# One-token attention with a gated feed-forward: how w_down, wo and V's last tiles are loaded

## The chip, the cores and the metric

The kernel runs on one core of one Trainium2 chip. The metric is device time in microseconds (us) of that core. Before the change the median of three runs is 2534.33 us (2534.22 to 2534.78).

## What is computed

One token `x` (512 values, bf16) goes through two branches that are mixed by a scalar gate.

```python
q  = (x @ wq)                        # 32 heads of 128
s  = q . k_cache[h, :, :] * 128**-0.5  # 65536 keys a head
o  = softmax(s) @ v_cache[h]           # [32, 128]
a  = o.reshape(1, 4096) @ wo           # wo: 4096 x 512
b  = (silu(x @ w_gate) * (x @ w_up)) @ w_down   # w_down: 1792 x 512
g  = sigmoid(sum(x * gate_w))
out = g * a + (1 - g) * b
```

K and V hold 32 heads x 65536 x 128 bf16 values each: 512 MiB each. The weights are small beside them: wq 4 MiB, wo 4 MiB, w_gate, w_up and w_down 1.75 MiB each.

## The kernel before

**Tiles.** The caches are read in tiles of 16384 keys (4 MiB, 32 KiB on each of 128 partitions): four K tiles and four V tiles a head, 128 of each in all. Five buffers ("slots") of that size lie in SBUF; `take` hands out the slot that has been free the longest and `give` returns one. K tiles, V tiles and the larger weights all go through these five slots, so the order of `take` and `give` in the program decides which transfer waits for which reader.

**Work on a tile.** For a K tile, VectorE multiplies by the query (L254) and adds halves (L258), TensorE adds the rest up with the identity as weights (`scores`, L267), and VectorE folds that into the scores (L281). After four K tiles a head's maximum and exponentials are made (`row_max`, `exponentials`). For a V tile, TensorE runs 32 matmuls `O_ps<-V_t,P_sb` (`values`, L322), four blocks of 128 keys each. When a head's four V tiles are done, `head_copy` (ScalarE, L335) and `head_turn` (TensorE L351, ScalarE L358) turn the result into a column of `oT`, and `project` (L365) multiplies that with the head's 128 rows of wo into two accumulators `a_ps`. In the last V tile the last eight blocks (`TURNED`) are multiplied the other way round, straight into `oh_ps` (L343), behind everything else.

**Order.** All loads but two tiny ones are issued by SyncE, in the order of the program, with eight completion semaphores that are used in turn. The order at the start is: the first part of wq, K tiles 0, 1, 2, the rest of wq, w_gate, K tile 3, w_up, then six DMAs of w_down, K tile 4, two more DMAs of w_down, V tile 0. From K tile 5 on, a step issues one K and one V tile (`steps`); V is four tiles behind K at first and from K tile 43 on falls back to eight (`LAG`, `SPREAD`), so that the run ends with V tiles alone.

**w_down before (L393 to L412).** It lies on 64 partitions, 28 rows of 512 values on each. It comes in eight DMAs of eight partitions each, and each partition's share is one run of 28,672 bytes. `feed_forward_out` first turns the hidden vector from 128x14 to 64x28 (L227, L231) and then runs 28 matmuls (L233).

**wo before.** Rows of heads 0 to 15 come four heads at a time (512 KB, in runs of 1 KB) in mid-run (`load_wo`, L163), into a pool of two buffers; rows of heads 16 to 31 (2 MB) come behind the last V tile in four DMAs (`load_late`, L169) into a ring slot. Heads 0 to 15 are projected in mid-run, heads 16 to 31 at the very end (L480).

**V's last tiles before.** `V_CUTS` cuts the third last tile and the second last in two DMAs each, and the last in six (32, 32, 32, 16, 8 and 8 blocks).

Of the kernel before, what the change touches and what calls it, by code (L numbers as in the profile page):

```python
# [8 lines left out]
ACT = mybir.ActivationFunctionType  # L9
ALU = mybir.AluOpType  # L10
AXIS = mybir.AxisListType
P = 128
# [3 lines left out]
NB = 128  # L16
# [6 lines left out]
LAG = 8  # L23
SPREAD = 40

WG = 4
LATE = 16
LATE_CUTS = (0, 5, 10, 14, LATE)
TURNED = 8
V_CUTS = {3: (0, 64, NB), 2: (0, 64, NB), 1: (0, 32, 64, 96, 112, NB - TURNED, NB)}  # L30


@with_exitstack
def kernel(
# [14 lines left out]
    nc = tc.nc  # L49
    bf16 = mybir.dt.bfloat16  # L50
    f32 = mybir.dt.float32

    _, H, Sk, Dh = A_k_cache.shape
    D = A_x.shape[2]
    F = B_w_gate.shape[1]
    KT = D // P
    FT = F // P
    G = Sk // (NB * P)
    NBH = Sk // P
    N = H * G  # L60
# [4 lines left out]
    consts = ctx.enter_context(tc.tile_pool(name="consts", bufs=1))  # L65
# [7 lines left out]
    psum_m = ctx.enter_context(tc.tile_pool(name="psum_m", bufs=2, space=bass.MemoryType.PSUM))  # L73
# [7 lines left out]
    def take(name):  # L81
        slot = free.pop(0)
        held[name] = slot
        return ring.tile(
            [P, NB * Dh], bf16, name=name.split(".")[0], tag=f"slot{slot}"
        )

    def give(name):
        free.append(held.pop(name))
# [14 lines left out]
    def load(dst, cache, n, name, cuts=(0, NB), slot=None):  # L104
        h, g = divmod(n, G)
        t = take(f"{name}.{n}") if slot is None else slot
        view = t.rearrange("p (j d) -> p j d", d=Dh)
        src = cache[0, h, g * NB * P : (g + 1) * NB * P, :].rearrange("(p j) d -> p j d", j=NB)
        for a, b in zip(cuts[:-1], cuts[1:]):
            nc.sync.dma_start(out=view[:, a:b, :], in_=src[:, a:b, :])  # L110
        dst[n] = view

    def load_k(n):
        load(K_tiles, A_k_cache, n, "K_t")

    def load_v(n):
        load(V_tiles, A_v_cache, n, "V_t", V_CUTS.get(N - n, (0, NB)))

# [9 lines left out]
    ident_b = consts.tile([P, P], bf16, name="ident_b")  # L128
# [29 lines left out]
    wo_tiles = {}  # L158

    def load_wo(g):  # L160
        wo_tiles[g] = wo_pool.tile([P, WG, D], bf16, name="wo_sb", tag="wo_sb")
        rows = A_wo[g * WG * P : (g + 1) * WG * P, :]
        nc.sync.dma_start(out=wo_tiles[g], in_=rows.rearrange("(h p) n -> p h n", p=P))  # L163

    def load_late(cuts):
        late = take("wo_late.0")[:, : LATE * D].rearrange("p (h n) -> p h n", n=D)
        rows = A_wo[(H - LATE) * P :, :].rearrange("(h p) n -> p h n", p=P)
        for a, b in zip(cuts[:-1], cuts[1:]):
            nc.sync.dma_start(out=late[:, a:b, :], in_=rows[:, a:b, :])  # L169
        return late  # L170

    def feed_forward_in():
        gu_ps = psum_m.tile([P, 2 * FT], f32, name="gu_ps", tag="misc")
        for w in range(2):
            cols = wgu_sb[:, w].rearrange("p t (m c) -> p t c m", c=FT)
            for ft in range(FT):
                for t in range(KT):
                    nc.tensor.matmul(
                        gu_ps[:, w * FT + ft : w * FT + ft + 1],
                        lhsT=cols[:, t, ft, :],  # L180
                        rhs=xT[:, t : t + 1],
                        start=(t == 0),
                        stop=(t == KT - 1),
                    )
        gu_sb = consts.tile([P, 2 * FT], f32, name="gu_sb")
        nc.scalar.activation(out=gu_sb, in_=gu_ps, func=ACT.Copy)
        eg = consts.tile([P, FT], f32, name="eg")
        nc.scalar.activation(out=eg, in_=gu_sb[:, :FT], func=ACT.Exp, scale=-1.0)
        return gu_sb, eg
# [32 lines left out]

    def feed_forward_out(hT, rest):
        b_ps = psum_m.tile([1, D], f32, name="b_ps", tag="misc")
        h_ps = psum_m.tile([HP, GT], f32, name="h_ps", tag="misc")
        for r in range(2):
            nc.tensor.matmul(  # L227
                h_ps[:, r * FT : (r + 1) * FT], lhsT=ident_b[:, r::2], rhs=hT, start=True, stop=True
            )
        h2 = consts.tile([HP, GT], bf16, name="h2")  # L230
        nc.scalar.activation(out=h2, in_=h_ps, func=ACT.Copy)  # L231
        for t in range(GT):
            nc.tensor.matmul(  # L233
                b_ps, lhsT=h2[:, t : t + 1], rhs=wd_sb[:, t, :], start=(t == 0), stop=(t == GT - 1)
            )
        nc.scalar.activation(out=b_sb, in_=b_ps, func=ACT.Copy, scale=rest)
        for i, a in enumerate(a_ps):
            nc.tensor.matmul(  # L238
                a, lhsT=ones_f[0:1, 0:1], rhs=b_sb[:, i * HD : (i + 1) * HD], start=True, stop=False
            )  # L240
# [22 lines left out]
    def scores(n):  # L263
        S = F_tiles[n] = psum_s.tile([P, NB, QUAD], f32, name="S_ps")
        width = width_of(n)
        for c in range(0, width, QUAD):
            nc.tensor.matmul(  # L267
                S,
                lhsT=ident_b,
                rhs=K_tiles[n][:, :, c : c + QUAD],  # L270
                start=(c == 0),
                stop=(c == width - QUAD),
            )
        del K_tiles[n]
        give(f"K_t.{n}")
# [84 lines left out]
        )  # L360

    def project(h):
        rows = wo_tiles[h // WG][:, h % WG, :] if h < H - LATE else wo_late[:, h - (H - LATE), :]
        for i, a in enumerate(a_ps):
            nc.tensor.matmul(  # L365
                a,
                lhsT=oT[:, h : h + 1],
                rhs=rows[:, i * HD : (i + 1) * HD],
                start=False,
                stop=(h == H - 1),  # L370
            )


    def score_tile(n):
        for _ in products(n):
            pass
        if n:
            fold(n - 1)
# [11 lines left out]
    score_tile(1)  # L390
    xs = gate_sum()
    scores(1)
    wd_t = take("wd_t.0")  # L393
    HP = P // 2
    GT = F // HP
    wd_sb = wd_t[:HP, : GT * D].rearrange("p (t n) -> p t n", t=GT)
    wd_rows = B_w_down.rearrange("(p t) n -> p t n", t=GT)
    firsts = (0, 1, 2, 3, 32, 33, 34, 35)

    def load_wd(i):  # L400
        part = slice(firsts[i], firsts[i] + 29, 4)
        nc.sync.dma_start(out=wd_sb[part], in_=wd_rows[part])

    for i in range(6):
        load_wd(i)
    for g in range(1, H // QG):
        queries(g)
    give("wq_t.0")
    eg2 = gate_exp(xs)
    load_k(4)  # L410
    load_wd(6)
    load_wd(7)  # L412
    score_tile(2)
    rest = gate_value(eg2)
    scores(2)
# [7 lines left out]
    v = 0  # L423
# [5 lines left out]
        steps.append((None, v))  # L429
        v += 1  # L430

    done = tot_ps = wo_late = None
    for n, v in steps:
        if n is not None and n > G:
            load_k(n)
        if v is not None:
            if v % (WG * G) == 2 and v // (WG * G) < (H - LATE) // WG:
                load_wo(v // (WG * G))
            if v:
                load_v(v)  # L440
            if v == N - 1:
                wo_late = load_late(LATE_CUTS)
        vector = iter(()) if n is None else products(n)
        top_of = None
        if n is None:
            top_of = H - 1 if F_tiles else None
        elif n % G == 0:
            top_of = n // G - 1
            vector = (i for a in (0, NB // 2) for i in products(n, a, a + NB // 2))
        if top_of is not None:  # L450
            next(vector, None)
            fold(top_of * G + G - 1)
            mT_ps = row_max(top_of)
            next(vector, None)
            exponentials(top_of, mT_ps)
        if n == G:
            hT = feed_forward_mid(*ff)
        for _ in vector:
            pass
        if n is not None and n % G:  # L460
            fold(n - 1)
        if tot_ps is not None:
            weight(*tot_ps)
            tot_ps = None
        if n == G:
            feed_forward_out(hT, rest)
            give("wd_t.0")
        if done is not None:
            head_turn(done, head_copy(done))
        if v is not None:  # L470
            values(v)
        if top_of is not None:
            tot_ps = top_of, total(top_of)
        if n is not None:
            scores(n)
        if done is not None and done < H - LATE:
            project(done)
        done = v // G if v is not None and v % G == G - 1 else None
    head_turn(H - 1, head_copy(H - 1))
    for h in range(H - LATE, H):  # L480
        project(h)

    out_sb = consts.tile([1, D], bf16, name="out_sb")
    nc.vector.tensor_copy(out=out_sb[:, :HD], in_=a_ps[0])  # L484
# [32 lines left out]
```

## Time and profile before

| What | Value |
|---|---|
| Median of three runs | 2534.33 us |
| The profiled execution | 2534.41 us |
| Its span in the profile | 2532.6 us |
| Mean granted TensorE clock | 0.772 |
| Busy: TensorE, VectorE, ScalarE | 61%, 82%, 3% |
| Read from HBM | 1087.64 MB, 429 GB/s over the span |

The span starts with the first recorded instruction and ends with the last; 1.8 us of the profiled execution lie outside it. All bytes are input: the output is 1 KB. The DMA work is spread over 16 DMA engines, and a DMA has landed when each engine that carries a part of it has reported.

### The profile page before, as it was taken

The page shows a single profiled execution, that of the slowest core. Times are in us where ns is not written, and L with a number is a line of the kernel's source. Part 1 is how long each engine was busy: PE and PEld are TensorE (multiplying, and loading weights), DVE is VectorE, ACT ScalarE, POOL GpSimd, SP SyncE. Part 2 cuts the span into 40 slices and gives each one's busy share as a digit, 9 for nine tenths or more (in the row PEclk, how much of TensorE's full clock was granted, in tenths as well). Part 3 has the DMA queues.
Part 4 walks back from the last instruction along what each step waited for, and adds up shares of the span by engine and source line. Part 5 has one row for each costly group of instructions (what it writes and reads, how often), then busy time and mean ns, then how long its engine had stood idle before and what let it go on. Part 6 is the DMA issues. An engine that isn't in the chain of part 4 may idle for free.

```text
span 2532.6 us, 13195 instructions
## 1 busy us (share of the span) xinstructions
PE 1533.7 (61%) x5786; PEld 581.6 (23%) x5786; DVE 2083.7 (82%) x744; ACT 77.7 (3%) x208; POOL 0.9 (0%) x7
## 2 busy tenths in 40 slices
PE   4656656665566555555665566556656665665569
PEld 1222222222222112222222122222222221222223
DVE  7788888888887999988888888888888888888860
ACT  1000000000000000000000000000000000000000
POOL 0000000000000000000000000000000000000000
PEclk9777777777777787787777777777777777777779
DMA  9999999999999999999999999999999999999998
GB/s 412 418 431 433 435 432 430 434 433 432 431 433 434 431 433 434 432 431 434 433 432 433 434 432 432 435 431 432 432 434 432 431 435 433 431 434 433 432 432 351
DMA packets 43915, 1088.49 MB, mean 430 GB/s; under 512 B 4753, under 2 KB 9362, under 8 KB 10258
## 3 DMA queue, kind: packets, MB, share of 16 engines
q1 hardware_dynamic: 43570, 1087.65, 99.7%
q8 instruction: 45, 0.74, 0.1%
q14 instruction: 12, 0.10, 0.0%
q10 hardware_dynamic: 288, 0.00, 0.0%
HBM read 1087.64 MB, written 0.00 MB: 429 GB/s over the span
## 4 chain that ended last, share of the span: by engine, by line
DMA 71%; PE 23%; DVE 4%; issue 1%; ACT 0%; SPq 0%; DVEq 0%
DMA V_t<-in_A_v_cache_dram 63%; PE O_ps L322 21%; DMA K_t<-in_A_k_cache_dram 8%; DVE K_t L254 3%; DVE K_t L258 1%; PE S_ps L267 1%; DMA wo_late<-in_A_wo_dram 0%; PE b_ps L233 0%; DVE S_sb L281 0%; DVE m L287 0%; PE oh_ps L351 0%; PE a_ps L238 0%; ACT P_sb L300 0%; PE a_ps L365 0%; PE mT_ps L291 0%
## 5 line engine op out<-in xcount | busy, mean ns | idle before, releaser
L322 PE MATMUL O_ps<-V_t,P_sb 128*4 128x512 bf16 x4094 | 1154.5, 452 | 663.5 <-DMA V_t<-in_A_v_cache_dram 663.5
L254 DVE TENSOR_TENSOR K_t<-K_t,q_bc 128x16384 bf16<-128x16384 bf16 (+1 forms) x159 | 1117.2, 7026 | 357.9 <-DMA K_t<-in_A_k_cache_dram 346.7
L258 DVE TENSOR_TENSOR K_t<-K_t 128x8192 bf16<-128x8192 bf16 (+1 forms) x314 | 859.7, 2738 | 8.6
L322 PEld LDWEIGHTS <-P_sb 128*4 128x4 bf16 x4094 | 393.0, 97 | 1405.1 <-issue 1064.1
L267 PE MATMUL S_ps<-K_t,ident_b 128*128 128x512 bf16 x1056 | 263.3, 393 | 100.6 <-DVE K_t L258 100.6
L267 PEld LDWEIGHTS <-ident_b 128*128 128x128 bf16 x1056 | 98.0, 101 | 248.0 <-issue 158.0
L291 PE MATMUL mT_ps<-diag,ones_f 128*128 128x128 f32 x64 | 24.5, 483 | 150.1 <-ACT diag L289 150.1
L351 PE MATMUL oh_ps<-ident_f,O_sb 4*128 4x1 f32 x256 | 55.5, 334 | 74.5 <-ACT O_sb L335 74.5
L281 DVE TENSOR_REDUCE S_sb<-S_ps 128x128 f32<-128x512 f32 x128 | 87.5, 683 | 4.9 <-PE S_ps L267 4.9
L289 ACT ACTIVATE diag<-ident_f,m 128x128 f32<-128x128 f32 x32 | 12.8, 401 | 2118.7 <-DVE m L287 2118.7
L351 PEld LDWEIGHTS oh_ps<-ident_f,O_sb 4*128 4x128 f32 x256 | 52.8, 301 | 84.1 <-ACT O_sb L335 82.9
L291 PEld LDWEIGHTS mT_ps<-diag,ones_f 128*128 128x128 f32 x64 | 15.2, 295 | 166.7 <-ACT diag L289 166.7
L484 DVE CAST out_sb<-a_ps 1x256 bf16<-1x256 f32 x1 | 0.4, 412 | 56.6 <-PE a_ps L365 56.6
L300 ACT ACTIVATE P_sb<-S_sb,bias 128x512 bf16<-128x512 f32 x32 | 23.1, 722 | 1.0
L287 DVE TENSOR_REDUCE m<-S_sb 128x1 f32<-128x512 f32 x32 | 22.0, 686 | 1.1
L335 ACT ACTIVATE O_sb<-O_ps 4x512 f32<-4x512 f32 x32 | 18.3, 572 | 129.2 <-PE O_ps L322 129.2
L313 DVE RECIPROCAL recip<-tot_ps 128x1 f32<-128x1 f32 x32 | 5.1, 158 | 13.0 <-PE tot_ps L308 13.0
L308 PEld LDWEIGHTS tot_ps<-rowsum,ones_f 128*128 128x128 f32 x64 | 9.5, 188 | 14.0 <-issue 14.0
L233 PE MATMUL b_ps<-wd_t,h 64*1 64x512 bf16 x28 | 12.1, 625 | 0.3 <-ACT h L231 0.3
L308 PE MATMUL tot_ps<-rowsum,ones_f 128*128 128x1 f32 x64 | 12.2, 260 | 0.0
L358 ACT ACTIVATE oT<-oh_ps,rg 128x1 bf16<-128x1 f32 x32 | 8.4, 263 | 65.0 <-PE oh_ps L351 65.0
L296 DVE TENSOR_REDUCE top<-mT_ps 128x1 f32<-128x128 f32 x32 | 9.1, 284 | 1.0 <-PE mT_ps L291 1.0
(47 smaller groups left out, 75.2 us busy)
## 6 DMA issues: line engine op xcount, KB each, us to landing
K_t<-in_A_k_cache_dram SPq DMA_DIRECT2D x128, 4096.0 KB, 35.3
V_t<-in_A_v_cache_dram SPq DMA_DIRECT2D x125, 4096.0 KB, 28.0
V_t<-in_A_v_cache_dram SPq DMA_DIRECT2D x4, 2048.0 KB, 31.1
wq_t<-in_A_wq_dram SPq DMA_DIRECT2D x1, 3584.0 KB
V_t<-in_A_v_cache_dram SPq DMA_DIRECT2D x3, 1024.0 KB
wo_sb<-in_A_wo_dram SPq DMA_DIRECT2D x4, 512.0 KB, 38.8
gu_t<-in_B_w_gate_dram SPq DMA_DIRECT2D x1, 1792.0 KB
gu_t<-in_B_w_up_dram SPq DMA_DIRECT2D x1, 1792.0 KB
```

The source lines that it names most:

```text
L254: yield nc.vector.tensor_tensor(out=K, in0=K, in1=q_rep, op=ALU.mult)
L258: yield nc.vector.tensor_tensor(out=K[:, :, 0:half], in0=K[:, :, 0:half], in1=K[:, :, half : 2 * half], op=ALU.add,)
L267: nc.tensor.matmul(S, lhsT=ident_b, rhs=K_tiles[n][:, :, c : c + QUAD], start=(c == 0), stop=(c == width - QUAD),)
L281: nc.vector.tensor_reduce(out=S_tiles[h][:, g * NB : (g + 1) * NB], in_=F_tiles.pop(n), axis=AXIS.X, op=ALU.add)
L287: nc.vector.tensor_reduce(out=m, in_=S_tiles[h], axis=AXIS.X, op=ALU.max)
L289: nc.scalar.activation(out=diag, in_=ident_f, func=ACT.Copy, scale=m)
L291: nc.tensor.matmul(mT_ps, lhsT=ones_f, rhs=diag, start=True, stop=True)
L300: nc.scalar.activation(out=P_tiles[h], in_=S_tiles[h], func=ACT.Exp, bias=bias, scale=scale, accum_out=rowsum[:, h : h + 1],)
L308: nc.tensor.matmul(tot_ps, lhsT=ones_f, rhs=rowsum[:, h : h + 1], start=True, stop=True)
L322: nc.tensor.matmul(O_tiles[h], lhsT=P_tiles[h][:, g * NB + j : g * NB + j + 4], rhs=V_tiles[n][:, j : j + 4, :], start=(g == 0 and j == 0) ...
L335: nc.scalar.activation(out=O_sb, in_=O_tiles.pop(h), func=ACT.Copy)
L351: nc.tensor.matmul(oh_ps, lhsT=O_sb[:, c * Dh : (c + 1) * Dh], rhs=ident_f[0:4, c : c + 1], start=(c == 0 and not turned), stop=(c == 3),)
```

## The change

w_down comes as one DMA on 128 partitions (14 rows of 512 values on each, 14,336 bytes in one run), issued behind K tile 4 instead of before and behind it; the hidden vector is used as it lies, with 14 matmuls. wo comes two heads at a time (256 KB), sixteen DMAs in mid-run, for all 32 heads; each head but the last is projected in mid-run, and nothing of wo is loaded behind V. The second last V tile comes in four DMAs of 32 blocks, the last in seven (32, 32, 16, 16, 16, 8 and 8 blocks). Because K tile 4 is now taken ahead of w_down, K tile 4 gets the slot that K tile 1 had, and w_down the slot that wq had.

```diff
-WG = 4
-LATE = 16
-LATE_CUTS = (0, 5, 10, 14, LATE)
+WG = 2
 TURNED = 8
-V_CUTS = {3: (0, 64, NB), 2: (0, 64, NB), 1: (0, 32, 64, 96, 112, NB - TURNED, NB)}
+V_CUTS = {3: (0, 64, NB), 2: (0, 32, 64, 96, NB), 1: (0, 32, 64, 80, 96, 112, NB - TURNED, NB)}
...
-    def load_late(cuts):
-        late = take("wo_late.0")[:, : LATE * D].rearrange("p (h n) -> p h n", n=D)
-        rows = A_wo[(H - LATE) * P :, :].rearrange("(h p) n -> p h n", p=P)
-        for a, b in zip(cuts[:-1], cuts[1:]):
-            nc.sync.dma_start(out=late[:, a:b, :], in_=rows[:, a:b, :])
-        return late
...
     def feed_forward_out(hT, rest):
         b_ps = psum_m.tile([1, D], f32, name="b_ps", tag="misc")
-        h_ps = psum_m.tile([HP, GT], f32, name="h_ps", tag="misc")
-        for r in range(2):
-            nc.tensor.matmul(
-                h_ps[:, r * FT : (r + 1) * FT], lhsT=ident_b[:, r::2], rhs=hT, start=True, stop=True
-            )
-        h2 = consts.tile([HP, GT], bf16, name="h2")
-        nc.scalar.activation(out=h2, in_=h_ps, func=ACT.Copy)
-        for t in range(GT):
-            nc.tensor.matmul(
-                b_ps, lhsT=h2[:, t : t + 1], rhs=wd_sb[:, t, :], start=(t == 0), stop=(t == GT - 1)
+        for t in range(FT):
+            nc.tensor.matmul(
+                b_ps, lhsT=hT[:, t : t + 1], rhs=wd_sb[:, t, :], start=(t == 0), stop=(t == FT - 1)
             )
...
-        rows = wo_tiles[h // WG][:, h % WG, :] if h < H - LATE else wo_late[:, h - (H - LATE), :]
+        rows = wo_tiles[h // WG][:, h % WG, :]
...
-    for i in range(6):
-        load_wd(i)
     for g in range(1, H // QG):
         queries(g)
     give("wq_t.0")
     eg2 = gate_exp(xs)
     load_k(4)
-    load_wd(6)
-    load_wd(7)
+    wd_t = take("wd_t.0")
+    wd_sb = wd_t[:, : FT * D].rearrange("p (t n) -> p t n", t=FT)
+    nc.sync.dma_start(out=wd_sb, in_=B_w_down.rearrange("(p t) n -> p t n", t=FT))
     score_tile(2)
...
-            if v % (WG * G) == 2 and v // (WG * G) < (H - LATE) // WG:
+            if v % (WG * G) == 2:
                 load_wo(v // (WG * G))
             if v:
                 load_v(v)
-            if v == N - 1:
-                wo_late = load_late(LATE_CUTS)
...
-        if done is not None and done < H - LATE:
+        if done is not None:
             project(done)
...
-    for h in range(H - LATE, H):
-        project(h)
+    project(H - 1)
```

More of the change, by code (lines that the diff above doesn't have):

```diff
@@ L392 @@
     scores(1)
[L393 to L402, printed above, removed]
-    for i in range(6):
-        load_wd(i)
     for g in range(1, H // QG):
@@ L430 @@
         v += 1
-    done = tot_ps = wo_late = None
+    done = tot_ps = None
     for n, v in steps:
```

## The prediction

> **What bounds the kernel now.** I read the page's slices first, then the chain that ended last, then the start and the end of the run.
>
> ```profile
> span 2532.6 us, 13195 instructions
> PE 1533.7 (61%) x5786; PEld 581.6 (23%) x5786; DVE 2083.7 (82%) x744; ACT 77.7 (3%) x208; POOL 0.9 (0%) x7
> ...
> DMA  9999999999999999999999999999999999999998
> GB/s 412 418 431 433 435 432 430 434 433 432 431 433 434 431 433 434 432 431 434 433 432 433 434 432 432 435 431 432 432 434 432 431 435 433 431 434 433 432 432 351
> ...
> DMA 71%; PE 23%; DVE 4%; issue 1%; ACT 0%; SPq 0%; DVEq 0%
> ```
>
> The DMA engines are full in every slice at about 433 GB/s; the chain is DMA with TensorE's reads between. All bytes must come anyway, so only the first two slices, the last one, and how evenly the 16 engines are loaded can move the time.
>
> The start, from the timeline: six w_down DMAs, K tile 4, two more; then K tile 4's multiplication, late by 7.72 us with nothing to explain it.
>
> ```profile
> 46.38 4.19 SPq L402 DMA_DIRECT2D wd_t<-in_B_w_down_dram  x6
> ...
> 57.01 0.34 SPq L110 DMA_DIRECT2D K_t<-in_A_k_cache_dram  x1
> ...
> 62.34 1.71 SPq L402 DMA_DIRECT2D wd_t<-in_B_w_down_dram  x2
> ...
> 78.44 4.42 DVE L254 TENSOR_TENSOR K_t<-K_t,q_bc 128x8192 bf16<-128x8192 bf16 x1 [7.72 <-issue]
> ...
> 100.10 0.33 SPq L110 DMA_DIRECT2D K_t<-in_A_k_cache_dram  x1
> ```
>
> The trace also records when each DMA engine reports its part of a DMA. This is my extract (us; number of reports, first, last):
>
> ```text
> w_gate          16 reports  46.75   47.27
> K tile 3        16          56.45   56.94
> w_up            16          60.70   62.33
> w_down 1 of 8    9          47.54   63.39
> w_down 6 of 8    9          50.98   68.70
> K tile 4        16          70.52   78.36
> w_down 8 of 8    9          64.48   80.49
> V tile 0        16          80.24   90.15
> K tile 5        16          89.91   99.81
> K tile 6        16         112.27  119.45
> last V piece    16        2509.92 2523.84
> last wo piece   16        2525.57 2529.27
> ```
>
> Ahead of w_down, whole tiles are reported by 16 engines within 0.6 us. A DMA of w_down has nine reports, one at once and eight data parts; after them K tile 4 falls into two groups of eight, 6 to 8 us apart. So w_down went through eight engines only, and these carry everything behind it late; the slot of a tile comes free only when the slowest engine has reported. The other eight wait for issues at 100 us (K tile 6 is issued at 100.10). Successive last reports of whole tiles then stand 9.68 us apart to the end, on an engine that never pauses; the spread between first and last report grows to 13.9 us by steps of 1.4 us, each with one 16 KB instruction packet of another queue.
>
> The end, from the chain:
>
> ```profile
> 2486.99 29.42 DMA V_t<-in_A_v_cache_dram
> 2516.40 0.02 issue
> 2516.42 12.18 DMA wo_late<-in_A_wo_dram
> 2528.60 0.04 issue
> 2528.65 1.48 PE a_ps L365 x12
> 2530.13 0.02 issue
> 2530.15 0.37 ACT out_sb L485
> ```
>
> The end hangs on the last wo piece (2529.27), not on V. From there to the span's end are 3.33 us. So the time is: **the slowest DMA engine's last report plus the tail behind it.** Each step is priced on these two.
>
> **w_down.** The last reports of the first six w_down DMAs are 1.06 us apart (63.39 to 68.70): eight cost the slow engines 8.5 us. As one DMA in runs of 14,336 bytes it has w_gate's shape, and w_gate took 47.27 - 42.96 (end of wq) = 4.31 us. Check: w_up to K tile 5 is 99.81 - 62.33 = 37.48 us; three tiles and 4.31 are 33.35. That is **-4.1 us**. Bounds: -4.3 at best; -2.6, half of the 5.1 us by which the two groups stay apart from 130 us on; nothing at all is a rival below. After 100 us, V tile 1, K tile 6 and the first wo took 9.78, 9.86 and 1.65 us instead of 9.68, 9.68 and 1.34, while the early engines burst back in: 0.6 us, of which I take half, **-0.3** (0 to -0.6).
>
> [...]
>
> Moved order: K tile 4 waits only for K tile 1's slot (scores done near 46.4) and is issued there, not at 57.01. w_down is issued behind it when the queries have read wq (52.2); V tile 0 waits behind it on SyncE, but for K tile 2's scores (60.1) anyway. Queued data then ends near 76 us, so no engine runs dry. K tile 4's multiplication starts near 72 us. The 28 matmuls of 0.43 us and the turn (12.7 us) become 14 (6.0); K tile 6 is issued near 87 us instead of 100, long before its turn (105). These gains on VectorE and TensorE are worth nothing by themselves: data is late, not they. Without the DMA's cover they would be 6 to 7 us each.
>
> **wo.** The same bytes in the same 1 KB runs. Four mid-run pieces cost the slowest engine 1.34 us each (undisturbed), the 2 MB at the end 2529.27 - 2523.84 = 5.43: 10.79 in all. Sixteen of 256 KB at 0.67 (the last piece, 2529.27 - 2528.60) are 10.72: **-0.1** (0.3 either way). The wait for a free wo buffer is over: the head that used it was projected ten V tiles before. Behind wo stands a V tile on SyncE that has some 28 us from issue to landing; twelve more issues of 0.43 us disappear in that. The 15 heads' projections in mid-run are 30 short matmuls beside a TensorE that waits 663 us for V.
>
> [...]
>
> **V's pieces.** The second last tile: 4 x 2.45 instead of 2 x 4.87, +0.06. In the last, one piece of 32 blocks (2.44) becomes two of 16 (1.26 each), +0.08. Together **+0.15** (0 to 0.3).
>
> **The tail.** Now the last V piece ends the loading. Pieces of 32 blocks land 2.44 us apart, and TensorE needs 8 x 0.221 = 1.77 (row: 32 matmuls in 7.07 us at 2514.00), so it has caught up: its last O_ps matmul ends at about the last landing L. Then, by the rows of before: L343 to L351 took 2524.46 to 2525.27 (0.81, O_sb's copy lies in it); L351 to the end of the oT copy 2525.27 to 2526.61 (1.34); two projections at 0.123 (12 in 1.48) and two hand-overs, 0.35; from TensorE's end to the span's end 2532.6 - 2530.13 = 2.47. Sum 4.98, against 3.33: **+1.65** (1.2, if hand-overs overlap, to 3.0, if TensorE comes 1.3 late).
>
> **Sum:** -4.1 - 0.3 - 0.1 + 0.15 + 1.65 = -2.7. Last landing near 2524.9, span 2529.9. Against the profiled 2534.41 (0.08 from the median 2534.33) this is 2531.7 us, -0.1%: within 0.2% (5.1 us, which I take as what a measurement here tells from no change). All bounds at their best give -4.1 (2530.3), at their worst +0.9 (2535.3); two of them bad at once, w_down and the tail, make 2534.6. With 0.3 us between runs I keep 2529.9 to 2534.6.
>
> **Rivals.**
> - *w_down frees nothing*, because it was level already or another engine ends as late: the first term is 0, 2535.8 us. [...] For it: the 45 instruction packets come round in eights by their durations, so several engines carry six of them and could be the next to end last. Against: one of the eight w_down engines ends last now, with its six packets already in the 2529.27; an engine with as many and an even share of w_down ends 4 us earlier. 5%.
> - *The end counts in bytes.* In the last 8 us before 2526 the windows show 285 and 228 GB/s. If 2.1 MB there cost 9.2 us and in mid-run 4.8, 4.4 more are won: 2527.3, faster. Against: the slowest engine took these 2 MB in 5.43 us without a pause; the low rate is of engines that had finished. 5%.
> - *TensorE falls to half clock between the smaller pieces* and ends last. A matmul then takes 0.427 us (as L322's at 2446), a quarter 3.4 us against 2.44 of landing: from the second last tile on it ends 11.2 us behind L, and L351 takes 1.86 instead of 1.05. Result 2543.8, slower. It decides once TensorE ends over 2.7 us behind L. For it: after waits of 8.7 us the granted clock was 0.66 at 2440 to 2455. Against: the gaps are 0.65 us, and after one of 1.06 at 2513 the clock stayed 1.00. 4%.
> - *Each added DMA is paid from issue to landing*: the smallest input, xT, took 1.8 us, four such are 7.2, and the time 2538.9, slower. [...] It would need a pause between the reports of V's pieces; none is seen. 2%.
>
> My forecast gets 84%; its own tails put 1% each beyond 0.2%. Faster 0.06, same 0.88, slower 0.06.
>
> **What will show it.** K tile 4's reports within 2 us of each other and its multiplication near 72 us; no split into two groups of eight; the chain ending V_t, O_sb, oh_ps, one projection; 16 wo loads with 0.67 us between last reports; granted clock 1.00 to the end. I am wrong if tile-to-tile steps leave 9.68 us, if the last V landing is not near 2524.9, or if more than 5.5 us follow it.

## The result and the profile after

The changed kernel takes 2542.64 us (median of 7 runs, 2542.18 to 2542.72) against 2534.22 us before (7 runs beside it, 2533.98 to 2534.85): ratio 1.0033 with a 95% interval of 1.0022 to 1.0044. It is slower by 8.4 us; the forecast was 2531.7 us. The page of the changed kernel:

```profile
span 2540.9 us, 13151 instructions
...
DMA  9999999999999999999999999999999999999998
GB/s 412 429 429 432 429 432 430 431 431 431 432 430 431 432 430 432 432 429 433 428 433 432 430 431 430 432 430 431 430 432 430 430 432 431 430 432 430 432 430 353
...
DMA 72%; PE 22%; DVE 5%; issue 0%; ACT 0%; SPq 0%; DVEq 0%; ACTq 0%
```

The second slice rose from 418 to 429 GB/s, which is the w_down part. But the slices behind it read 430 where they read 433 before, all through the run, with engines as full as before: the stream itself is slower. In two long stretches where nothing but the wo loads and projections differs (from 400 and from 1000 us) the windows of before and of after end in granted clock, DMA share and GB/s. First before:

```profile
core 0: us, PE busy (x) PEld busy (x) DVE busy (x) ACT busy (x) POOL busy (x), PEclk, DMA share, GB/s
400.00:1000.00 600.00, 351.54 (x1294) 131.40 (x1294) 519.83 (x184) 17.07 (x47) 0.00 (x0) 0.76 1.00 432
1000.00:2000.00 1000.00, 601.08 (x2211) 225.70 (x2211) 854.24 (x304) 29.31 (x81) 0.00 (x0) 0.77 1.00 433
```

then after:

```profile
400.00:1000.00 600.00, 355.58 (x1292) 131.73 (x1291) 517.85 (x182) 15.85 (x44) 0.00 (x0) 0.75 1.00 431
1000.00:2000.00 1000.00, 600.62 (x2220) 225.03 (x2220) 847.32 (x297) 27.16 (x76) 0.00 (x0) 0.77 1.00 431
```

The difference is small in these views; the single DMA packets in the trace show it better. A tile is 128 packets of 32 KB, eight on each DMA engine. My extract:

```text
                       packets of 32 KB: median  mean    at most 1214 ns   whole tiles, step between last reports
before                                   1213    1214.4       99%            9.680 us
after                                    1215    1218.2       16%            9.716 us
```

Some 250 steps by 0.036 us are 9 us, which is the size of the loss. It touches tiles of K and V that the change does not name.

The start did what was forecast. SyncE's timeline and VectorE's line for K tile 4:

```profile
46.84 0.33 SPq L108 DMA_DIRECT2D K_t<-in_A_k_cache_dram  x1
52.89 0.33 SPq L384 DMA_DIRECT2D wd_t<-in_B_w_down_dram  x1
60.44 0.33 SPq L108 DMA_DIRECT2D V_t<-in_A_v_cache_dram  x1
...
87.06 0.33 SPq L108 DMA_DIRECT2D K_t<-in_A_k_cache_dram  x1
```

```profile
72.39 4.42 DVE L238 TENSOR_TENSOR K_t<-K_t,q_bc 128x8192 bf16<-128x8192 bf16 x1 [1.30 <-DMA K_t<-in_A_k_cache_dram]
```

K tile 4 is issued at 46.84, multiplied from 72.39 (78.44 before), and K tile 5 has landed at 96.28 instead of 99.81 in spite of the slower packets. The end, from the chain of the changed kernel:

```profile
2518.12 16.17 DMA V_t<-in_A_v_cache_dram
2534.30 0.04 issue
2534.34 1.47 PE O_ps L306 x6
...
2535.90 0.59 ACT O_sb L319
...
2536.53 1.06 PE oh_ps L335 x8
...
2537.62 0.27 ACT oT L342
...
2537.94 0.39 PE a_ps L349 x2
```

It ends on V's pieces, O_sb, oh_ps and one projection, as foreseen; only it does so 10 us later. The last V piece has landed at 2535.61, not near 2524.9.

**What moved the tiles.** The program's memory layout shows a difference that the description of the change does not mention: h2, the turned hidden vector of 56 bytes a partition, lay ahead of the five ring slots, with only the output tile between. Without it, everything behind it moves down by 64 bytes. The slots started at byte 30976 of a partition, which is 121 x 256; now they start at 30912, which is 192 above a multiple of 256. Each slot is 32768 bytes long, so all five have the same remainder.

### The profile page after: what moved, and what is told of

It reads as the page before. It is cut to its first block, busy times and chain, and to the rows that moved or that the text cites. A ratio compares the mean times of both kernels' runs of the same rounds, so it can differ in the third digit from the quotient of the medians.

```text
span 2540.9 us, 13151 instructions
## 1 busy us (share of the span) xinstructions
PE 1535.7 (60%) x5769; PEld 580.5 (23%) x5770; DVE 2083.8 (82%) x744; ACT 77.5 (3%) x207; POOL 0.9 (0%) x7
## 4 chain that ended last, share of the span: by engine, by line
DMA 72%; PE 22%; DVE 5%; issue 0%; ACT 0%; SPq 0%; DVEq 0%; ACTq 0%
DMA V_t<-in_A_v_cache_dram 65%; PE O_ps L306 21%; DMA K_t<-in_A_k_cache_dram 7%; DVE K_t L238 3%; DVE K_t L242 2%; PE S_ps L251 1%; DVE S_sb L265 0%; PE oh_ps L335 0%; DVE m L271 0%; ACT P_sb L284 0%; ACT O_sb L319 0%; PE mT_ps L275 0%; DVE top L280 0%; ACT diag L273 0%; PE a_ps L349 0%
## 5 line engine op out<-in xcount | busy, mean ns | idle before, releaser
L349 PE MATMUL a_ps<-wo_sb,oT 128*1 128x256 bf16 x64 | 12.4, 275 | 0.4 <-ACT oT L342 0.4
```

## The experiments

**Theory A:** packets cost more when the slots do not start on a multiple of 256 bytes. **Theory B:** with w_down spread evenly, the 16 DMA engines stay in step and hinder each other. **Theory C:** sixteen wo loads and more V pieces disturb the stream.

**1. The changed kernel, slots back in place.**

```diff
         b_ps = psum_m.tile([1, D], f32, name="b_ps", tag="misc")
+        consts.tile([P, 2 * FT], bf16, name="pad")
```

> The changed kernel with one unused tile of 56 bytes a partition put where h2 was, so that the five ring slots start at byte 30976 of a partition again (as before) and not at 30912. Nothing else changes. Theory A (place of the slots: every 32 KB packet takes 2 to 9 ns longer when the slots do not start on a multiple of 256 bytes; whole tiles 9.71 us apart instead of 9.68): packets of 1213 ns again, tiles 9.68 us apart, about 2532 to 2533 us. Theory B (even loading by w_down leaves the 16 DMA engines in step, and they hinder each other): no difference, 2542.6 us. Theory C (16 small wo loads and more V pieces disturb the stream): no difference, 2542.6 us.

Measured: 2532.12 us against 2534.14 before (ratio 0.9993, 0.9983 to 1.0002). A tile that nothing reads or writes takes 10.5 us off the changed kernel. Median packet 1213 ns, 99.6% at most 1214, steps of 9.672 us. In the two traces the loss grows evenly: the changed kernel's last reports stand 0.3 us behind experiment 1 at K tile 5, 3.6 at K tile 50, 8.5 at K tile 110 and 10.0 at V tile 124. Theory A holds for these two places; B and C fall, since even loading and all small loads are still there. Its page, where the slices are back at about 433:

```profile
span 2530.5 us, 13152 instructions
...
GB/s 413 431 431 435 430 434 431 433 433 432 433 432 433 434 431 434 431 433 431 433 432 435 431 434 430 435 430 434 432 433 433 431 433 432 434 431 434 432 434 355
```

**2. The kernel before, slots moved.**

```diff
-        h2 = consts.tile([HP, GT], bf16, name="h2")
+        h2 = small.tile([HP, GT], bf16, name="h2")
```

> The kernel before with h2 moved to the pool behind the ring, so that the slots start at byte 30912 as in the changed kernel; all DMAs, their order and the matmuls stay. Theory A: the slowdown comes without the change, some 256 tiles by 0.037 us = 9.5 us, about 2543.5 us. Theories B and C: 2534.2 us, as before.

Measured: 2542.63 us (ratio 1.0034, 1.0021 to 1.0047), steps of 9.711 us, median packet 1215 ns. With every DMA as before, the move alone costs 8.5 us, against the 10.5 us of experiment 1. That the changed kernel's net loss is 8.4 us too is chance: there the move eats gains of 2 us. Part of the difference lies at the start: in the traces experiment 2 is 1.2 us ahead of the kernel before at K tile 4 and 7.7 us behind at V tile 124. Why it starts ahead no run tells; experiment 4, whose start is also as before, is 1.4 us ahead there.

**3. The w_down part alone, slots in place.** In the kernel before:

```diff
-        h2 = consts.tile([HP, GT], bf16, name="h2")
...
-        for t in range(GT):
...
+        consts.tile([P, 2 * FT], bf16, name="pad")
+        for t in range(FT):
...
-    for i in range(6):
-        load_wd(i)
...
     load_k(4)
-    load_wd(6)
-    load_wd(7)
+    wd_t = take("wd_t.0")
+    wd_sb = wd_t[:, : FT * D].rearrange("p (t n) -> p t n", t=FT)
+    nc.sync.dma_start(out=wd_sb, in_=B_w_down.rearrange("(p t) n -> p t n", t=FT))
```

> The kernel before with the w_down part alone (one DMA on 128 partitions behind K tile 4, 14 matmuls), and the unused tile that keeps the slots at byte 30976; wo and V's pieces as before. Theory A: only the gain of the w_down part, 3.5 to 4.4 us, 2529.9 to 2530.7 us. Theory B: the engines stay in step, tiles 9.71 us apart, and the loss of 9.5 us eats the gain: 2537 to 2540 us. Theory C: 2530 us.

Measured: 2530.01 us (0.9984, 0.9975 to 0.9994): 4.1 us faster than before, and the fastest of all whole kernels. Steps of 9.666 us. The gain is made at the start and kept: in the traces K tile 5 is reported 4.1 us earlier than before, V tile 124 4.6 us. Its page, whose second slice shows the gain:

```profile
span 2527.9 us, 13151 instructions
...
GB/s 414 428 434 434 433 431 432 432 433 435 432 431 432 433 434 433 432 432 432 433 433 433 433 432 432 434 434 432 432 433 435 433 432 432 432 436 434 431 431 371
```

**4. The wo part alone, slots in place.** The kernel before with two heads a load for all heads, `load_late` and the late projections taken out as in the change.

> The kernel before with the wo part alone (16 loads of two heads in mid-run, none at the end); w_down and V's pieces as before, slots at byte 30976. Theory A: tiles 9.68 us apart; the longer tail behind the last V piece costs 1.6 to 2.4 us, 2535.8 to 2536.6 us. Theory B: the same. Theory C: tiles further apart or each wo load over 0.7 us, 2540 us or more.

Measured: 2535.78 us (1.0008, 0.9998 to 1.0017), steps of 9.680 us. 1.6 us over the kernel before in the median, as forecast, though the interval touches no change: the ten runs fall into two groups, 2535.1 to 2535.2 and 2536.4 to 2537.0, and the median lies between them.

**5 and 6. Other places.** Experiment 3 with a larger unused tile.

```diff
-        consts.tile([P, 2 * FT], bf16, name="pad")
+        consts.tile([P, 60], bf16, name="pad")
```

> The w_down part alone, with the unused tile made larger so that the slots start at byte 31040 (64 above a multiple of 256). Theory A1 (what counts is a multiple of 256 bytes at the start of each packet's run in SBUF): slow like 30912, tiles 9.71 us apart, 2538.5 to 2539.5 us. Theory A2 (only the one place 30912 is bad, for instance against another tile): 2530 us.

Measured: 2540.22 us (1.0025, 1.0015 to 1.0034), steps of 9.713 us.

With 92 columns instead of 60:

> The same with the slots at byte 31104 (128 above a multiple of 256). Theory A1: slow, tiles 9.71 us apart, 2538.5 to 2539.5 us. Theory A3 (a multiple of 128 is enough): 2530 us.

Measured: 2539.94 us (1.0023, 1.0013 to 1.0033), steps of 9.714 us, though the median packet was 1216 ns and 35% took at most 1214. Both are 10 us slower than the same kernel at 30976 (experiment 3), 0.7 and 0.4 us above the range expected. Remainders of 64 and 128 are about as bad as the 192 of the changed kernel; a multiple of 128 is not enough. No other multiple of 256 than 30976 was tried; it is not a multiple of 512.

**7 and 8. Loads alone.** All stages are taken out; 100 tiles of K and V go into the five slots. An unused tile sets the place of the slots: 6720 columns for 30976, 6688 for 30912.

```diff
+    consts.tile([P, 6720], bf16, name="pad")
...
+    for n in range(100):
+        t = ring.tile([P, NB * Dh], bf16, name="K_t", tag=f"slot{n % SLOTS}")
...
+        nc.sync.dma_start(out=t.rearrange("p (j d) -> p j d", d=Dh), in_=src)
```

> Loads alone: 100 tiles of 4 MiB of K and V in turn into five slots that start at byte 30976; all computation is left out, so the output is zeros with five copied values. Each load waits only for the load that had its slot. All theories: packets of 1213 ns, tiles 9.67 to 9.68 us apart, a span of about 975 us.

> The same loads alone into slots that start at byte 30912; all computation is left out here too. Theory A1w (the write into SBUF itself costs more, whoever else works): tiles 9.71 us apart, packets of 1215 to 1222 ns, span 3.5 us longer than with slots at 30976. Theory A1r (the loads lose only where engines read or write tiles at such places): packets of 1213 ns, tiles 9.68 us apart, the same span.

Measured: 975.55 and 978.94 us, one run each. The pages, first with the slots at 30976:

```profile
span 973.8 us, 153 instructions
...
GB/s 394 435 440 431 432 431 431 431 433 436 439 435 432 431 431 431 432 435 435 440 432 432 431 431 431 433 436 436 436 432 432 431 431 431 433 436 440 432 433 366
```

and at 30912:

```profile
span 977.2 us, 153 instructions
...
GB/s 400 437 429 429 429 429 429 432 439 435 433 429 429 429 429 431 436 436 436 429 429 429 429 429 435 437 437 429 428 431 429 429 431 437 432 437 429 431 429 365
```

The common slice falls from 431 to 429 GB/s with no engine computing. So it needs no work of TensorE or VectorE; what differs between the two runs is the place in SBUF that the loads write: 3.4 us in 100 tiles, 800 packets on each DMA engine, so 4.2 ns a packet.

**9 and 10. The same loads in runs of 8 KB.**

```diff
-        nc.sync.dma_start(out=t.rearrange("p (j d) -> p j d", d=Dh), in_=src)
+        view = t.rearrange("p (j d) -> p j d", d=Dh)
+        for a in range(0, NB, 32):
+            nc.sync.dma_start(out=view[:, a : a + 32, :], in_=src[:, a : a + 32, :])
```

> The loads alone as in the earlier run into slots at byte 30976 (all computation left out), but each tile in four DMAs with runs of 8192 bytes: four times as many packets, the same bytes. Both theories: packets of 307 to 309 ns, quarters 2.43 to 2.45 us apart, about 982 to 986 us.

> The same four DMAs a tile into slots at byte 30912 (all computation left out). Theory F (a fixed extra for every run that does not start on a multiple of 256 bytes, some 4 ns): four times the loss of whole tiles, 13 to 14 us over the aligned twin. Theory S (a share of the bytes, 0.35%): again about 3.4 us.

Measured: 988.10 and 1001.78 us, one run each. The pages, first with the slots at 30976:

```profile
span 986.3 us, 454 instructions
```

and at 30912:

```profile
span 1000.0 us, 454 instructions
```

The aligned one is 2 us over its expectation; the difference, 13.7 us, is four times 3.4. So the price is paid for each run (4.3 ns on each of 3200 on every DMA engine) and is not a share of the bytes. The packet records give nearly the same: a packet of 32 KB takes 3.6 ns longer in the mean, one of 8 KB 4.7 ns.

The cost does not grow with the remainder: remainders of 64, 128 and 192 cost 10.2, 9.9 and 10.5 us (experiments 5, 6 and 1; 8.5 us for 192 in experiment 2). Nor is it the same for all packets: of the 32 KB packets of the changed kernel 50% took 1215 ns and 20% took 1222, 2 and 9 above the 1213 of before. What makes a packet longer at these places is not shown; the sources stayed, only the place in SBUF moved.

## Why the prediction was wrong

The step that failed is a silent one: that the tiles which the change does not name keep their steps of 9.68 us, so that the other terms can be added to the old stream. The sum costed the turn of the hidden vector by its instructions (the 28 matmuls and the turn) and put at nothing, without a reason, what else goes when h2's tile goes. That is a move of every slot by 64 bytes: +10.5 us (2542.64 - 2532.12). The terms that the sum has came out nearly as forecast. None of the rivals named the move. The text's own condition did: "I am wrong if tile-to-tile steps leave 9.68 us". They went to 9.716.

Point by point, on experiment 1, where that term is taken out (2532.12 against the forecast 2531.7):

- *w_down, -4.1 and -0.3.* Right, and 0.3 us too large together: experiment 3 gives -4.1 us (2530.01 - 2534.14). The two groups of eight are gone: K tile 4 is reported within 2.1 us. The early engines no longer pause: K tile 6 is issued at 87.19, and the first reports of K tile 5, V tile 1 and K tile 6 come 9.68 us apart.
- *wo, -0.1.* Right in size: the last reports of mid-run wo loads in experiment 1 stand 0.63 to 0.73 us behind those of the K tile ahead of them, 0.66 in the median, against the 0.67 that was used.
- *V's pieces, +0.15.* Right: in experiment 1 the four quarters step by 2.43, 2.42, 2.44 and 2.47 us and the two new pieces by 1.24 and 1.32, together 0.14 over two halves of 4.87 and a piece of 2.44.
- *The last landing, 2524.9.* Experiment 1: 2525.13.
- *The tail, 4.98.* Experiment 1: 2530.5 - 2525.13 = 5.37. TensorE's steps from its timeline:

```profile
2523.94 1.46 PE L307 MATMUL O_ps<-V_t,P_sb 128*4 128x512 bf16 x6 [0.18 <-DMA V_t<-in_A_v_cache_dram]
2525.33 0.35 PE L328 MATMUL oh_ps<-P_sb,V_t 128*128 128x1 bf16 x8
2526.14 1.05 PE L336 MATMUL oh_ps<-ident_f,O_sb 4*128 4x1 f32 x8 [0.46 <-ACT O_sb L320]
2527.54 0.38 PE L350 MATMUL a_ps<-wo_sb,oT 128*1 128x256 bf16 x2 [0.35 <-ACT oT L343]
```

  The hand-over of 0.81 and the next of 1.34 came as taken from before; TensorE starts L328 0.2 behind the last landing, and its end to the span's end took 2.58 instead of 2.47.
- *TensorE at half clock (4%).* Did not come: the granted clock was 1.00 in the windows of the changed kernel from 2480 to 2535 us, and its last O_ps matmul ended 0.2 us behind the last landing, not over 2.7. That its 2543.8 us lies nearest to the measured time is chance.
- *The end counts in bytes (5%)* and *each added DMA is paid from issue to landing (2%).* Both fall with experiment 1, which has every moved byte and every added DMA and lies within 0.5 us of the sum without them. The second's 2538.9 us has the direction right for a wrong reason.

So whether the change is faster or slower turned on something that costs nothing to keep. The version that beats both kernels is experiment 3: w_down as one DMA, wo left at the end, where its last pieces cover the work behind the last V piece, and 64 bytes of padding.

What stays open: in the shifted kernels most packets of the first tiles take no longer than with the slots in place. With loads alone they lengthen from about 44 us on (with runs of 8 KB from 15 us on), in the changed kernel from 57 us on, and why not from the first packet no run here tells. Nor is it shown why some packets pay 2 and others 9 ns, nor why the same move costs 8.5 us in one kernel and 10.5 in another.

One more thing moved with the slots. The 45 packets of 16 KB that bring instructions, and no tile, take 934 to 936 ns in the median in the four whole kernels with slots at 30976 (before, experiments 1, 3 and 4), but 1071 to 1074 ns in the four with shifted slots (the changed kernel, experiments 2, 5 and 6). So the price is not paid by the moved tiles alone; how it reaches these packets is not shown.

## What to carry to other kernels

Where DMA engines never pause, a price of about 4 ns a packet adds up over the some 2000 packets of each engine, so look where the big buffers start: a removed or added small tile moves all that is allocated behind it (here 56 bytes a partition, and all five slots by 64). Compare the memory layout of both versions, not only the instructions, and measure where the buffers of a stream start: of the four places measured here, byte 30976 (121 x 256) cost least, and 30912, 31040 and 31104 cost 8.5 to 10.5 us more in 2530. When a change is slower than the sum of its parts, look first at work that it did not touch.

## What the runs showed of the hardware

- With nothing computed, loads into slots at byte 30912 (192 above a multiple of 256) took about 4 ns more per run than into slots at 30976: 978.94 against 975.55 us for 100 tiles in runs of 32 KB (4.2 ns), 1001.78 against 988.10 in runs of 8 KB (4.3 ns). Starts at 64 and 128 above were measured in a whole kernel alone: 10.2 and 9.9 us in 2530.
- The eight w_down DMAs of the kernel before, over eight partitions each, loaded eight of the 16 DMA engines (nine reports, one of them 1.0 to 1.2 us after the issue, in place of 16). These engines stayed behind while all were full (the two groups start their reports 5.1 us apart from 130 us on), and a tile was used behind the last report (K tile 4 at 78.36, VectorE from 78.44). One DMA on 128 partitions in their place took 4.1 us off (experiment 3), for 1.75 MiB of w_down.
- 45 instruction packets of 16 KB are in a run. In the traces of before and after, the spread between first and last report of whole tiles jumps five times, each time with such a packet in the same 20 us: by 1.5 to 1.7 us (before) or 0.9 to 1.0 (changed kernel). In all it grows in the changed kernel from 1.6 us at K tile 4 to 9.6 at the end, and in the kernel before, with its eight-partition loads, from 6.9 us near 140 us to 13.9.
